# Products of 64 rows in pairs for QKV, output projection and the first FFN layer

## The chip, the core and the metric

The kernel runs on one core of a Trainium2 chip. The metric is the device time of one execution in microseconds. In the runs before the change the median was 483.98 us (two runs, 482.85 and 485.1).

A core has these engines: TensorE (PE in the profile; its weight loads are listed apart, as PEld), VectorE (DVE), ScalarE (ACT), GpSimd (POOL) and SyncE (SP), which here issues nearly all DMAs. TensorE multiplies a stationary operand, which a weight load puts into its array, with a moving operand that streams through, and adds the products up in banks of PSUM. The rows of the array are the contraction: 128 of them, which can be used as one group, as two of 64, or as four of 32.

## What is computed

One transformer layer over 2048 tokens of width 576, all tensors in bf16:

- x is normalised over its width (no gain, no offset) and multiplied with wq, wk, wv (576x576 each). There are 32 heads of 18.
- The tokens form four segments of 512. Inside a segment attention is causal: `softmax(q k^T * 18^-0.5 + mask) v`. In addition each segment reads a memory M, z that is built from all segments before it, with `phi(t) = t+1 if t>0 else exp(t)`: `a_mem = phi(q) M / (phi(q) z + 1e-6)`. Output of a head: `g * a_mem + (1-g) * a_dot`, with `g = sigmoid(beta)`.
- `h = x + o @ wo`.
- `out = h + gelu(layernorm(h) @ w1 + b1) @ w2 + b2`, with w1 576x4608 and w2 4608x576.

576 is four and a half times 128.

## The kernel before

**Tiles and streams.** Tokens are cut into 8 chunks of 256 (`NCH`, `Q`), each of two tiles of 128. Python generators describe the work of each stage; each yields what it has to wait for (`need`, L336) and then queues operations with `op` (L112):

- `stream_P(tl)` (L347, one for each of the two tiles): load x, layernorm (L303), transpose the normalised tile into `xT` (by TensorE for the first two chunks, by DMA afterwards), QKV in four blocks of 432 columns (L372 to L392), then the transposes of q and k.
- `stream_M` (L434): the memory of a chunk.
- `stream_A` (L565): attention in 80 visits. In a visit `scores` (L481) makes 16 products in groups of 32 rows into the four PSUM banks `st4`, ScalarE takes one exponential over all four banks into a buffer `pt` (L495), GpSimd masks (L499), and `weighted` (L510) multiplies with the values into the bank `ox` (L518). The value products of a visit are queued behind the scores of the next one.
- `stream_B(tl)` (L610): transpose the attention output `o_nat`, output projection in two blocks of 288 columns, add x, layernorm, transpose into `xn2T`.
- `stream_F1` (L690): the first FFN layer. For each pair of 128 hidden units one bank takes two blocks of 256 tokens (five products each), then DVE copies the bank to `hT` (L733). ScalarE's gelu follows over many units at once (L741).
- `stream_F2` (L748): the second FFN layer, 36 products of 288 columns into one bank (L767).

**A contraction over 576.** `mm5` makes it in five products, the last one with 65 live rows:

```
for k in range(4):
    nc.tensor.matmul(out=out_ap, lhsT=lhsT_of(slice(0, P), k), rhs=rhs_of(slice(0, P), k), start=(k == 0), stop=False)
nc.tensor.matmul(out=out_ap, lhsT=lhsT_of(slice(0, KTAIL), 4), rhs=rhs_of(slice(0, KTAIL), 4), start=False, stop=True)
```

In the profile the first four are L300 and the last is L301. Row 65 is a row of ones times b1 in the first FFN layer, and zeros elsewhere. QKV, output projection and first FFN layer all go through it.

**Weights.** wq, wk, wv and wo are loaded once (`weights`, L233: one DMA of 512 rows onto 128 partitions and one of 64 rows). w2 stays in SBUF. w1 is loaded anew for each chunk, in 9 groups of 512 columns, into two buffers (five for the first chunk): `load_w1` (L675) issues three DMAs per group, 512 KB, 64 KB and the 1 KB row of b1, when the group two before it has been used.

**Banks.** PSUM has eight banks here: four in `st4` for the scores, `ox`, and three that P, B, M, F1 and F2 share through `Slots` (L154). `ox` joins these three before and after the attention.

**What sets the order.** A planner in the kernel (L64 to L152, L776 to L819) plays the whole program through at build time, with a duration for each operation, a rate for DMA, and a due time from the table `SLACK` (L69). DVE, ACT, POOL and SP take the operation that is ready and due first. TensorE takes the first stream that is ready, in the order `stream_B`, `stream_A`, `stream_P`, `stream_M`, then F1 and F2, whichever is behind (L794 and L795); when the FFN lags, it comes first. What results is a fixed list of instructions for each engine, each queue in order; on the chip nothing is reordered. While F1 hasn't begun and TensorE has nothing to do, the planner puts in filler products (L805).

## Time and profile before

| what | value |
|---|---|
| median of the runs | 483.98 us (482.85 to 485.1) |
| profiled execution, first to last instruction (span) | 481.9 us, 2.1 us less than the median; what lies around the span is not in the profile |
| TensorE busy | 471.6 us, 98% of the span; mean granted clock 0.996 |
| DVE, ACT, POOL busy | 283.4, 290.0, 206.8 us |
| first FFN layer, QKV, output projection: L300 and L301, products | 308 blocks, 64 blocks, 32 blocks of five |
| score blocks (L489) | 80 of 16 products |
| DMA | 80.97 MB, 67 w1 loads of 512 KB and 5 more into `hT` for the first chunk; 64 transposing DMAs |
| first L300 of the first FFN layer | about 45 us |
| last first-layer product | about 458 us |

The profile is one execution. In the rows for groups a line reads: line of the kernel, engine, operation, output and input by name, shapes, count, then busy time of the group, mean of one, and idle time before them with what ended it. Products overlap in the pipeline, so the mean duration of one is longer than the distance from its start to the next one's. In the timeline each row is a run of equal instructions: start of the first, time to the end of the last, engine, line, shapes, count.

### The profile page before, as it was taken

Reading aid. Unit: us, or ns where it says so; the run is one execution under the profiler, and the core shown is the slowest. Engines: PE = TensorE matmul, PEld = TensorE weight load, DVE = VectorE, ACT = ScalarE, POOL = GpSimd, SP = SyncE. Lnnn points to the kernel's source line nnn. Section 1 sums busy time; section 2 is a strip of 40 time slices with the busy share of each in tenths; the row PEclk is TensorE's granted clock in tenths of the full one; section 3 lists DMA queues with packets and bytes.
Section 4 is the critical chain, followed back from the end, with each engine's and each line's share of the span. In section 5 each row is a group of like instructions: output and inputs, shape, how many; then the busy total and the mean of one; then the engine's idle time right before and its main releaser. Section 6 shows DMA issues by size and latency. Waiting matters only on the chain.

```text
span 481.9 us, 14443 instructions
## 1 busy us (share of the span) xinstructions
PE 471.6 (98%) x6098; PEld 369.1 (77%) x6098; DVE 283.4 (59%) x688; ACT 290.0 (60%) x205; POOL 206.8 (43%) x291
## 2 busy tenths in 40 slices
PE   8999999799999999999999999999999999999997
PEld 5668778467788878676887878768888778888885
DVE  5798776757776647676546654857534643534311
ACT  2678889763786969468237968658546867122210
POOL 6567552666755246776204353677304251100000
PEclk9999999899999999999999999999999999999999
DMA  8993759576894657499854655787854655755411
GB/s 237 291 337 113 172 147 252 112 139 163 164 215 147 167 160 197 107 197 232 191 174 125 168 152 153 160 145 172 221 171 130 149 151 155 194 173 161 135 38 50
DMA packets 117345, 80.97 MB, mean 168 GB/s; under 512 B 56392, under 2 KB 115232, under 8 KB 117280
## 3 DMA queue, kind: packets, MB, share of 16 engines
q1 hardware_dynamic: 117248, 80.04, 65.9%
q8 instruction: 48, 0.79, 0.7%
q14 instruction: 17, 0.14, 0.1%
q0 software_dynamic: 32, 0.01, 0.1%
HBM read 60.10 MB, written 7.08 MB: 139 GB/s over the span
## 4 chain that ended last, share of the span: by engine, by line
PE 88%; DMA 7%; DVE 2%; SPq 1%; ACT 1%; POOL 0%; issue 0%; ACTq 0%; DVEq 0%; POOLq 0%
PE bank L300 36%; PE bank L767 26%; PE bank L301 9%; PE ox L518 6%; PE st L489 5%; DMA xT<-xn 2%; DMA x_p<-in_A_x_dram 2%; PE ox L767 2%; DMA wqkv<-in_A_wv_dram 2%; PE ox L300 1%; DMA w1g<-in_B_b_dram 1%; ACT pt L495 1%; PE bank L447 1%; PE bank L541 1%; PE bank L805 1%; DMA xT<-o_nat 1%
## 5 line engine op out<-in xcount | busy, mean ns | idle before, releaser
L495 ACT ACTIVATE pt<-st 128x2048 bf16<-128x2048 f32 x80 | 150.2, 1878 | 61.9 <-PE st L489 61.6
L767 PE MATMUL bank<-w_sb,hT 128*128 128x288 bf16 x1080 | 155.7, 286 | 0.0
L300 PE MATMUL bank<-xn2T,w1g 128*128 128x256 bf16 (+1 forms) x1040 | 146.3, 269 | 0.0
L733 DVE CAST hT<-bank 128x512 bf16<-128x512 f32 x126 | 86.7, 690 | 86.9 <-PE bank L301 85.8
L767 PEld LDWEIGHTS <-hT 128*128 128x128 bf16 x1152 | 109.6, 98 | 27.9 <-issue 0.8
L499 POOL TENSOR_SCALAR_AFFINE_SELECT pt<-pt 128x512 bf16<-128x512 bf16 x128 | 81.0, 646 | 82.5 <-ACT pt L495 81.9
L300 PEld LDWEIGHTS <-w1g 128*128 128x128 bf16 x1104 | 101.4, 97 | 17.0
L741 ACT ACTIVATE hT<-hT 128x4608 bf16<-128x4608 bf16 (+3 forms) x22 | 65.9, 2996 | 67.1 <-DVE hT L733 67.0
L301 PE MATMUL bank<-xn2T,w1g 65*128 65x256 bf16 (+1 forms) x260 | 70.4, 271 | 0.1
L300 PE MATMUL bank<-wqkv,xT 128*128 128x432 bf16 x252 | 57.2, 349 | 2.6 <-DMA xT<-xn 2.1
L300 PEld LDWEIGHTS <-xT 128*128 128x128 bf16 x384 | 34.8, 98 | 27.1 <-DMA xT<-xn 2.4
L518 PEld LDWEIGHTS <-pt 128*128 128x128 bf16 x1280 | 43.6, 96 | 5.8 <-POOL pt L499 0.2
L518 PE MATMUL ox<-v_aug,pt 128*128 128x19 bf16 x1280 | 45.8, 172 | 0.1
L563 POOL TENSOR_TENSOR o_nat<-t,t 128x288 bf16<-128x288 f32 x24 | 19.6, 815 | 32.4 <-DVE t L562 32.2
L489 PE MATMUL st<-QT,KT 32*128 32x128 bf16 x1280 | 32.2, 217 | 0.7 <-ACT pt L495 0.7
L533 POOL TENSOR_TENSOR pq<-ek,pq 128x512 bf16<-128x512 bf16 x24 | 28.1, 1170 | 10.2 <-DVE ek L531 8.3
L771 DVE TENSOR_TENSOR ot<-bank,hc 128x288 bf16<-128x288 f32 x30 | 13.7, 457 | 30.0 <-PE bank L767 29.2
L489 PEld LDWEIGHTS <-KT 32*128 32x128 bf16 x1280 | 18.6, 92 | 14.7 <-issue 12.9
L301 PEld LDWEIGHTS <-w1g 65*128 65x128 bf16 x276 | 26.9, 97 | 3.5 <-DMA w1g<-in_B_b_dram 0.4
L317 POOL TENSOR_TENSOR rstd_b<-rstd_b,mhalf 128x1 f32<-128x1 f32 x16 | 8.8, 552 | 44.6 <-DVE rstd_b L312 44.6
L383 ACT CAST qk_pad<-bank 128x432 bf16<-128x432 f32 x31 | 15.9, 522 | 16.9 <-PE bank L301 12.6
L637 DVE TENSOR_TENSOR h_t<-bank,x_b 128x288 f32<-128x288 f32 x32 | 14.6, 457 | 13.5 <-PE bank L301 13.1
(99 smaller groups left out, 499.8 us busy)
## 6 DMA issues: line engine op xcount, KB each, us to landing
w1g<-in_B_w_dram SPq DMA_DIRECT2D x67, 512.0 KB
w_sb<-in_B_w_dram SPq DMA_DIRECT2D x6, 864.0 KB
hd<-h_t SPq DMA_DIRECT2D x16, 288.0 KB
hc<-hd SPq DMA_DIRECT2D x32, 144.0 KB
w1g<-in_B_w_dram SPq DMA_DIRECT2D x67, 64.0 KB
x_b<-in_A_x_dram SPq DMA_DIRECT2D x18, 144.0 KB
hT<-in_B_w_dram SPq DMA_DIRECT2D x5, 512.0 KB
out_dram<-ot SPq DMA_DIRECT2D x16, 144.0 KB
```

The lines of the kernel that those rows point to most:

```text
L300: nc.tensor.matmul(out=out_ap, lhsT=lhsT_of(slice(0, P), k), rhs=rhs_of(slice(0, P), k), start=(k == 0), stop=False)
L301: nc.tensor.matmul(out=out_ap, lhsT=lhsT_of(slice(0, KTAIL), 4), rhs=rhs_of(slice(0, KTAIL), 4), start=False, stop=True)
L383: op("ACT", 0.52, lambda ch=ch, uh=uh, qk=qk: nc.scalar.copy(out=qk[:, 24 * ch:24 * ch + 24, 0:Dh], in_=uh), [b], [(*qkk, ch)])
L489: nc.tensor.matmul(out=st4[:, i, n * P:(n + 1) * P], lhsT=KTs[(c - c % 2 + kt // 2) % 3][rows, g, (kt % 2) * P:(kt % 2 + 1) * P], rhs=QTs[ ...
L495: op("ACT", 1.88, lambda: nc.scalar.activation(out=pt[:], in_=st4[:], func=ACT.Exp, scale=scale), sk, [("pt", slot, n) for n in range(4)], ...
L499: op("POOL", 0.65, lambda n=n: nc.gpsimd.affine_select(out=pt[:, :, n * P:(n + 1) * P], in_=pt[:, :, n * P:(n + 1) * P], pattern=[[0, 4], ...
L518: nc.tensor.matmul(out=oxv[:, 4 * (g % 4) + i, :], lhsT=pts[slot][:, i, n * P:(n + 1) * P], rhs=v_augs[(2 * s0 + kt) % 6][:, 4 * g + i, :] ...
L533: op("POOL", 1.16, lambda: nc.gpsimd.tensor_tensor(out=pq[:], in0=e_g, in1=pq[:], op=ALU.add), ["ek"], ["pq"], slack=SLACK["add"])
L563: op("POOL", 0.8, lambda: nc.gpsimd.tensor_tensor(out=o_dst, in0=t1[:], in1=t2[:], op=ALU.add), ["t1", "t2"], ok, slack=SLACK["sum"])
L733: op("DVE", 0.684, lambda hT=hT, jp=jp, acc=acc: nc.vector.tensor_copy(out=hT[:, 2 * jp:2 * jp + 2, :], in_=acc), [b], [("hT", c % 2, jp)] ...
L741: op("ACT", (f1 - f0) * Q * 0.00083 + 0.18, lambda hT=hT, f0=f0, f1=f1: nc.scalar.activation(out=hT[:, f0:f1, :], in_=hT[:, f0:f1, :], fun ...
L767: nc.tensor.matmul(out=acc, lhsT=hT[:, q, tl * P:(tl + 1) * P], rhs=w2_sb[:, q, hs], start=(q == 0), stop=(q == NF - 1))
```

## The change

- `mm5` goes. Its successor `lanes` makes nine steps of two products, the lower product on partitions 0 to 63, the upper on 64 to 127. Each half has its own result and its own bank: half 0 takes one set of output columns, half 1 another, and both contract over all of 576 in nine pieces of 64 rows. The upper half takes the pieces in another order of storage (`xs`).
- For this, xT and xn2T hold each 64-row piece of the transposed activations on both halves (9 slots of 128 columns where there were 5). The tile to be transposed gets its first 64 columns once more behind its last (`layernorm` writes twice, POOL copies for `o_nat`), and each DMA transpose becomes two, of 5 and of 4 blocks (`spread_t`); where TensorE transposes, ACT copies the even slots and DVE twice the odd ones (`spread`).
- QKV becomes three pairs of 288 columns (q on half 0 and k on half 1, twice, and v in two halves), the output projection one pair, the first FFN layer a pair for each 256 of 512 hidden columns. The biases b1 are no row of the product any more; the eviction adds them (`tensor_tensor` in place of `tensor_copy`).
- w1 is loaded by two DMAs of 288 KB, each onto 64 partitions, with rows of 512 bytes where they had 1024. The other weights are laid out in the same way.
- The four score banks may be taken by the other streams. A visit of attention begins when all four are free.
- The planner knows a tiling for each operation (32, 64 or 128) and adds 0.095 us where it changes; its choice for TensorE is by tiling (below). Nearly all of `SLACK` has new values.
- `pt` has two buffers for three, xn2T three for four. The load of x and the layernorm of the next chunk are queued when the current tile has been transposed. The gates of beta are computed earlier.

Second FFN layer, scores, value products, gelu and memory stay.

The core of the diff:

```diff
+    def lanes(outs, weight, moving):
+        for k in range(KB):
+            for h in range(2):
+                xs = k if h == 0 else (k - 1) % KB
+                nc.tensor.matmul(out=outs[h], lhsT=weight(half(h), k, xs), rhs=moving(half(h), k, xs), start=(k == 0), stop=(k == KB - 1))
...
+        def apply():
+            for to, n in ((0, D), (D, HB)):
+                nc.vector.tensor_scalar(out=dst[:, to:to + n], in0=src[:, 0:n], scalar1=mv[:, 0:1], scalar2=rstd[:],
+                                        op0=ALU.subtract, op1=ALU.mult)
...
+    def spread(bank, b, dst, key):
+        pt = bf16v(bank[:])[:, 0:KT * P].rearrange("p (k q) -> p k q", q=P)
+        op("ACT", 0.69, lambda: nc.scalar.copy(out=dst[:, 0:KB:2, :], in_=pt), [b], [key])
+        for h in range(2):
+            op("DVE", 0.4, lambda h=h: nc.vector.tensor_copy(out=dst[half(h), 1:KB:2, :], in_=pt[half(1 - h), h:h + 4, :]), [b], [(*key, h)])
+
+    def spread_t(dst, src, rd, wr, slack):
+        for o in range(2):
+            n = KT - o
+            dma_t(n, dst[:, o:KB:2, :], src[:, o * HB:o * HB + n * P], rd, wr[o:o + 1] if o == 0 else wr[1:], slack)
...
+            for pr in range(3):
+                wk = ["wq", "wk"] if pr < 2 else ["wv0", "wv1"]
+                xk3 = [kx, (*kx, 0), (*kx, 1)]
+                yield need(None, bank_slots, xk3 + wk, mode=64, n=2)
+                bs = [bank_slots.take() for _ in range(2)]
+                accs = [banks[b][:, 0:NH] for b in bs]
+                op("PE", KB * mm(NH), lambda pr=pr, accs=accs, xTt=xTt: lanes(
+                    accs, lambda r, k, xs: xTt[r, xs, :], lambda r, k, xs: wqkv[r, k, pr * NH:(pr + 1) * NH]), xk3 + wk, bs, mode=64)
...
+        def again():
+            if gh == 0:
+                o_t = o_nats[c % 2][:, qt, :]
+                op("POOL", 0.2, lambda: nc.gpsimd.tensor_copy(out=o_t[:, D:XW], in_=o_t[:, 0:HB]), ok, [("oe", c % 2, qt)], slack=slack if c < 2 else SLACK["sum"])
...
-        dma(512, lambda: nc.sync.dma_start(out=wt[:, 0:4, :], in_=B_w1[0:512, fcols].rearrange("(k p) f -> p k f", p=P)), (), [k], SLACK["w1"])
-        dma(64, lambda: nc.sync.dma_start(out=wt[0:64, 4, :], in_=B_w1[512:576, fcols]), (), [k + ("t",)], SLACK["w1"])
-        dma(1, lambda: nc.sync.dma_start(out=wt[64:KTAIL, 4, :], in_=b1_row[:, fcols]), (), [k + ("b",)], SLACK["w1"])
+        for h in range(2):
+            f0 = n % NG * 512 + h * Q
+            dma(288, lambda h=h, f0=f0: nc.sync.dma_start(out=wt[half(h), :, :], in_=B_w1[:, f0:f0 + Q].rearrange("(k r) f -> r k f", r=HB)),
+                (), [(*k, h)], SLACK["w1"])
...
+                for a in range(2):
+                    if a:
+                        yield need(mode=64)
+                    op("PE", KB * mm(Q), lambda accs=accs, a=a, wt=wt, c=c: lanes(
+                        [acc[:, a, :] for acc in accs], lambda r, k, xs: wt[r, k, a * P:(a + 1) * P],
+                        lambda r, k, xs: xn2T[c % NX][r, :, xs, :]), xks[0] + xks[1] + wk, bs, mode=64)
+                for h in range(2):
+                    f = 4 * fg + 2 * h
+                    op("DVE", 0.69, lambda hT=hT, f=f, acc=accs[h]: nc.vector.tensor_tensor(
+                        out=hT[:, f:f + 2, :], in0=acc, in1=bias(f, Q), op=ALU.add),
+                       [bs[h], "b1T"], [("hT", c % 2, f // 2)], slack=SLACK["evict"])
+                    bank_slots.give(bs[h])
...
+        if free_at["PE"] <= now:
+            best = {}
+            for g in [*first, *ffn]:
+                if g in waits and waits[g].idle and waits[g].mode not in best and waits[g]() <= now:
+                    if g is ffn[1] and work["F1"] > 0 and g is F1 and 64 in best:
+                        continue
+                    best[waits[g].mode] = g
+            if lead and 32 in best and len(best) > 1:
+                del best[32]
+            if best:
+                inside = now - entered
+                if tiling == 64:
+                    order = (64, 32, 128) if inside < SLACK["in64"] else (32, 64, 128)
+                elif tiling == 128:
+                    order = (32, 128, 64) if inside < SLACK["in128"] else (32, 64, 128)
+                else:
+                    order = (64, 128) if came == 128 else (128, 64)
```

In the new table `in64` is -53, so from the 64-row tiling scores are taken as soon as they are ready, and `in128` is 2.5 us.

## The prediction

> **What bounds the kernel now.** I read the page's busy shares first, then the chain that ended last, then the busy times by stage, and last the order of TensorE's instructions in a few microseconds. From the page:
>
> ```profile
> PE 471.6 (98%) x6098; PEld 369.1 (77%) x6098; DVE 283.4 (59%) x688; ACT 290.0 (60%) x205; POOL 206.8 (43%) x291
> ...
> PE 88%; DMA 7%; DVE 2%; SPq 1%; ACT 1%; POOL 0%; issue 0%; ACTq 0%; DVEq 0%; POOLq 0%
> ...
> L300 PE MATMUL bank<-xn2T,w1g 128*128 128x256 bf16 (+1 forms) x1040 | 146.3, 269 | 0.0
> ```
>
> TensorE is busy 98% of the span and holds 88% of the chain; no other engine passes 60%. Busy time alone could hide waits, so the stages come next (columns: length, then busy time of PE, PEld, DVE, ACT, POOL, clock, DMA share):
>
> ```profile
> 24.00:100.00 76.00, 72.17 (x1199) 55.01 (x1198) 57.92 (x142) 60.86 (x48) 42.52 (x60) 0.98 0.71 184
> 100.00:200.00 100.00, 100.00 (x1405) 78.20 (x1403) 67.40 (x170) 70.04 (x51) 58.24 (x81) 1.00 0.71 170
> 200.00:300.00 100.00, 99.92 (x1292) 77.73 (x1281) 57.84 (x142) 63.57 (x43) 43.23 (x56) 1.00 0.70 168
> 300.00:400.00 100.00, 99.53 (x1326) 78.53 (x1324) 56.96 (x138) 65.94 (x43) 45.85 (x63) 1.00 0.67 161
> ```
>
> From 100 to 400 us TensorE idles 0.55 us. Time taken off its stream there comes off the span, unless something else then comes late. Before about 45 us it is different: the filler products of L805 (70 of them, the last at 42.4 us) show that TensorE waits there for the first attention chunk.
>
> The mean of 269 ns for a product overlaps with its neighbours, so the true price is the distance between starts, from the timeline of PE:
>
> ```profile
> 207.27 0.30 PE L541 MATMUL bank<-MZ_blk,pq 128*128 128x76 bf16 x4
> 207.51 0.40 PE L489 MATMUL st<-QT,KT 32*128 32x128 bf16 x16
> 207.84 0.56 PE L518 MATMUL ox<-v_aug,pt 128*128 128x19 bf16 x16
> 208.26 0.89 PE L300 MATMUL bank<-wqkv,xT 128*128 128x432 bf16 x4
> 208.99 0.35 PE L301 MATMUL bank<-wqkv,xT 65*128 65x432 bf16 x1
> 209.17 0.60 PE L300 MATMUL bank<-xn2T,w1g 128*128 128x256 bf16 x4
> 209.61 0.27 PE L301 MATMUL bank<-xn2T,w1g 65*128 65x256 bf16 x1
> 209.72 0.60 PE L300 MATMUL bank<-xn2T,w1g 128*128 128x256 bf16 x4
> ```
>
> From 209.17 to 209.72 is one FFN block: five products of 256 columns in 0.55 us, the fifth with only 65 live rows but at full price. In the records of single products the steps are 109 ns at 256 columns, 122 at 288, 182 at 432, 55 at 128, and the step after a 65-row product is 4 to 5 ns longer.
>
> The score block (L489) is the only work in row groups. Its sixteen products start in four rounds of four; inside a round the starts lie 4 ns apart, and the last two rounds begin 56 ns after the one before. So four groups run at once, each into its own bank, for what one full product of 128 columns costs (55). It also shows what entering and leaving costs. L541's products stand 34 ns apart, so its four should give way at 207.41, but the scores start at 207.51; and the last score starts at 207.695, needs 56 ns, and L518 follows at 207.84. That is 96 ns in and 91 out (93 to 96 and 91 wherever scores border other work): 80 blocks, 160 switches, 15 us already in the span and counted as busy.
>
> **Part 1, products removed.** A contraction of 576 takes 5 passes now and 9 half passes, two at a time, afterwards (4.5).
> - First FFN layer: 268 blocks of 4x109+113 = 549 ns and 40 blocks of 128 columns of 280 ns, 158.3 us. After: 134 pairs of 9x109 = 981 ns and 20 of 9x55 = 495, 141.4.
> - QKV: 64 blocks of 4x182+187 = 915 ns, 58.6. After: 48 pairs of 9x122 = 1098, 52.7.
> - Output projection: 32 blocks of 4x122+126 = 614, 19.6. After: 16 of 1098, 17.6.
>
> 236.5 becomes 211.7: **24.8 us less**. Four QKV tiles (0.37 us each) and two output projections (0.13) lie in the head, where the chain of the first chunk and not TensorE's load decides: 1.7 us of this is not won, leaving 23.1.
>
> **Part 2, the price of a pair's step.** No 64-row pair runs in the trace. If both halves run like score groups, a step costs a full product plus 1 ns (56 against 55); a second start that isn't hidden costs 4. That is 0 to 7.5 us over 1872 steps. The score row is nearest: +1 ns, **+1.9**. The two-run operand of the first layer (two tiles of 128 columns) I put at nothing within the same bounds.
>
> **Part 3, more switches.** Now every block but the scores has one tiling, and the order between them is free. Afterwards FFN, QKV and output projection stand in the 64-row tiling, second layer and value products in the full one. Each score block must be followed by value products (128) before the next scores, so a stretch between two score blocks that also holds 64-row work has three switches where it had two. The trace has such work in 75 of 79 stretches. The new order in `step` collects one kind of work: after scores it goes to the kind it didn't come from, and it stays in the full tiling for 2.5 us. I take a quarter of the stretches as free of 64-row work, so 60 more there, and 30 more where no scores stand (the tail from 410 to 458 us, now 48 us of first and second layer in turn, and the pauses of 10 to 25 us between score bursts): 90 at 93 ns, **+8.4**. Bounds: 40 more (3.7) if blocks are well collected, 150 (14) if banks and w1's two buffers break them up.
>
> **Part 4, DMA.** The transposes for xT, o and xn2T are each split in two (5 and 4 blocks): 40 more issues of 1.21 us on SP's queue, and about 1.2 us later landing. w1 loses its bias row: 0.38+0.48+0.44 us of issue become two of some 0.48, 24 us less on SP. SP's 250 busy us become about 274, not a bound; but behind each extra transpose wait w1 and x loads. In the chain, xT<-xn holds two pieces (4.2 us at 88 and 5.7 us at 216) and x_p<-x two before them; TensorE stood idle 2.1 us for the first. There 1.2 us more may show twice; against that, the change issues the next chunk's x load and layernorm ahead of the QKV products. I take +0.5 for both together, from -2 (these waits go) to +8 (every landing late at the two places and the tail's loads too).
>
> w1 packets halve to 512 bytes. Median packet times are 18 ns at 256 bytes, 46 at 1024, 51 at 1152, so I estimate 28 at 512: 56 ns for what took 46, 22% more. Now 512 KB move in 1.9 us, and the whole load lands 3.2 us after its issue; then in about 4. In the tail, at today's 4.1 us per group, a buffer is free for two groups less the 2.0 us of its own products, 6.2 us. That covers it; packed closer, at 3 us per group, the 4.0 us left would just do.
>
> A weighed rule: 64 rows written by 64 packets of 1024 bytes (the tail of w1) took 0.25 us at 428.60, 46 ns each, like the full loads' packets. The Trainium skill, SBUF — State Buffer, section "Door 1: The DMA port swizzle", says that 64 rows reach half of the ports and measures 196 GB/s against 328. The trace's small piece doesn't agree (262 GB/s). By the row the sum stands; by the rule it is that of the fourth rival below.
>
> **Part 5, what is hidden.** Evictions with the bias: a PSUM add of 288 columns takes 457 ns (L637), a copy 456, so 690 at 512 as today. Layernorm's second write (32 times 0.15 to 0.3), `spread`'s copies (12 of about 0.4), POOL's 16 copies of about 0.2: beside TensorE, with DVE at 59%. In the head they sit on the chain, about 1 us, against gates moved earlier and two QKV pairs in place of three chunks ahead of the first scores: nothing. Two `pt` buffers suffice: on TensorE's queue the values of visit v-2 stand ahead of the scores of v. Three xn2T buffers too: the transposes of chunk c wait for the first layer of c-3 in place of c-4, and today that is done 49 us before the output projection of c, or more.
>
> **Sum.** -24.8+1.7+1.9+8.4+0.5 = -12.3: a span of 469.6 for 481.9. The runs' median is 483.98, 2.1 above that span; with the same 2.1 around it, **472**.
>
> **Rivals.**
> - *Switches and late landings eat most of it.* 150 switches, pairs at +4 ns, waits +4: -24.8+1.7+7.5+14+4 = +2.4, so 486; at half of the way from the sum above, 479. For: two w1 buffers cap a 64-row stretch at two groups (3.9 us). Against: the score banks add four to the FFN's. 478 to 490, chance 0.24.
> - *More is won.* 40 switches, waits -2, pairs at +0: -24.8+1.7+3.7-2 = -21.4, so 463; 457 to 464. For: the pauses without scores, where 64-row work can be gathered in few stretches. 0.13.
> - *Weight loads don't hide (slower).* In a pair, each half must load 64 rows while it streams. A load with a 19-column product costs 25 ns (L518); one such load open per step is 1872x25 = 47 us: 472+47 = 519. It decides from 12 ns per step (1872x12 = 22 us: the 12 us gain and 2% more). Against: in the scores, loads for a group start 10 ns after that group's product and four fit into a 56 ns round. 0.05. The Trainium skill, TensorE: Matmul & The Clock Gate, "The mechanism" in Part 3, says loads overlap running products only of other row groups; the score records don't agree.
> - *Half loads at half rate.* 576 KB then take about 4.3 us (512 KB now 1.9), 72 x 4.3 = 310 us of the queue beside 180 of others: over 490, some 500. The 46 ns packets speak against it. 0.05. This is where the rule of the Trainium skill's page SBUF — State Buffer would lead.
> - *The pairs don't overlap at all:* 1872 steps twice: over 600. 0.01.
>
> My forecast (464 to 478) keeps 0.52. Two per cent, about what a measurement tells from no change here, is 474.3 to 493.7. Faster: 0.13 and 0.40 of the forecast's 0.52, 0.53; slower 0.09 (unhidden loads 0.05, 0.03 of the half loads, the last 0.01); within, the other 0.38. Range 460 to 488: it leaves out some 0.07 below and 0.12 above.
>
> **What would show it.** The first layer's steps at 109 to 110 ns with two products each; the scores' neighbours still at 93 ns per switch; 220 to 310 switches in all; TensorE without gaps from 100 us on; the fillers ending near 42 us. Wrong if a pair's step is 115 ns or more, if w1 or xT appear among PE's waits with more than 5 us, or if switches pass 310.

## The result and the profile after

The changed kernel takes **555.68 us** (median of two executions, 555.14 to 556.22) against 483.98: 1.148 times the time before, with an interval of 1.143 to 1.153. The forecast was 472, the range 460 to 488. Span: 553.4 us against 481.9.

The page of the changed kernel: TensorE's row and the row of the clock, the row of the DMA engines in tenths, the hardware DMA queue (packets, MB, share of 16 engines' time), and the shares of the chain that ended last.

```profile
PE 490.8 (89%) x8049; PEld 378.8 (68%) x8049; DVE 290.5 (53%) x745; ACT 292.0 (53%) x225; POOL 207.7 (38%) x300
...
PEclk8999998799999899989999999999989799989999
DMA  8993989988499984986998986998875867997631
...
q1 hardware_dynamic: 181504, 85.22, 83.9%
...
PE 61%; DMA 13%; DVE 10%; ACT 5%; issue 4%; SPq 4%; POOL 2%; DVEq 0%; ACTq 0%; POOLq 0%
```

Before, TensorE was busy 98% of the span and held 88% of the chain. Now it is busy 89% and holds 61%; the shares of transfers (13%), VectorE (10%) and ScalarE (5%) have grown from 7, 2 and 1%, so TensorE waits. The queue's row says where to look first. Before, it read `q1 hardware_dynamic: 117248, 80.04, 65.9%`: the same data but for 6%, in 1.55 times as many packets, which keep the sixteen engines busy for 464 us (83.9% of 553.4) in place of 318. The row of tenths has slice after slice at 8 and 9.

The three stretches in which TensorE had 0.55 us without work before (length; busy time of PE, PEld, DVE, ACT, POOL; granted clock; DMA share; GB/s):

```profile
100.00:200.00 100.00, 84.40 (x1282) 63.87 (x1283) 55.45 (x135) 51.09 (x41) 37.27 (x50) 0.95 0.90 154
200.00:300.00 100.00, 88.98 (x1540) 70.06 (x1537) 59.07 (x159) 56.30 (x46) 50.01 (x71) 0.98 0.91 153
300.00:400.00 100.00, 92.71 (x1527) 71.50 (x1524) 49.75 (x119) 63.51 (x44) 39.21 (x55) 1.00 0.86 171
```

TensorE is idle 34 us of these 300. The DMA share was 0.71, 0.70 and 0.67 and is near 0.9, while the rate was 170, 168 and 161 GB/s and is 154, 153 and 171: the engines are busier and move about as much. What TensorE waited for (us in total, times, longest), by the page's view of waits:

```profile
PE bank L339 <- DMA w1g<-in_B_w_dram: 13.1, 12, 2.4
PE bank L339 <- DMA xT<-o_nat: 4.6, 4, 3.1
PE st L339 <- DMA xT<-o_nat: 3.6, 1, 3.6
PE bank L368 <- DVE xn L360: 3.5, 1, 3.5
PE st L339 <- DVE qk_pad L443: 3.2, 2, 2.6
PE bank L339 <- issue: 2.9, 2, 2.2
PE st L339 <- ACT qk_pad L441: 2.6, 4, 1.1
PE st L339 <- DMA w1g<-in_B_w_dram: 2.5, 4, 1.0
PE st L339 <- DVE hT L802: 2.2, 3, 0.8
```

L339 is the pair. All rows of this view together are 24.5 us for transfers, 20.5 for VectorE, 6.6 for ScalarE, 1.2 for GpSimd and 5.0 for "issue" (no cause that the profile shows); before they were 4.5, 1.5 and 0.7, and none for the last two. So there are two families: transfers that land late, and work of VectorE and ScalarE that isn't done in time, much of it the emptying of banks.

And the pairs themselves, in order of time:

```profile
303.78 0.40 PE L539 MATMUL st<-QT,KT 32*128 32x128 bf16 x16
304.11 2.14 PE L339 MATMUL bank<-xn2T,w1g 64*128 64x256 bf16 x36
306.18 0.56 PE L568 MATMUL ox<-v_aug,pt 128*128 128x19 bf16 x16
```

Thirty-six products of 256 columns, 18 steps of two, from 304.11 to the switch before 306.18: 109 ns a step. Over all steps inside pairs the median distance is 109 ns at 256 columns and 122 at 288, what one full product costs. The pairs do what they were made for.

**The account.** To see where 71 us went I price the distances between starts on TensorE, as the prediction did: a step by the distances measured there (55, 109, 122 and 182 ns at 128, 256, 288 and 432 columns, that is 0.417 ns a column plus 2.4 ns; 25 ns for the products of 19 columns), a switch 94 ns; a longer distance is a wait, and one about twice its price, inside a run of equal products, is the halved clock. In us:

| | products and fillers | switches | waits | halved clock, missing records | rest | first to last start |
|---|---|---|---|---|---|---|
| before | 445.9 | 160: 15.0 | 9.3 | 2.2 | 4.7 | 477.1 |
| after | 431.4 | 286: 26.9 | 73.9 | 12.9 | 3.5 | 548.5 |
| difference | -14.5 | +11.9 | **+64.6** | **+10.7** | -1.2 | +71.4 |

The halved clock goes with the waits. In the records of the clock the kernel before has one stretch at 0.5 before its end (3.4 us), the changed kernel eight, of 3.4 or 6.8 us. Each of the eight begins during a wait of TensorE or within 2 us of its end; these waits are 0.6 to 3.6 us long. Not every long wait has one: behind 3.1 us that end at 172.4 there is none for 12 us. One of the eight, in the tail:

```profile
487.94 3.44 PE L339 MATMUL bank<-xn2T,w1g 64*128 64x256 bf16 x35 [2.40 <-DMA w1g<-in_B_w_dram]
```

After 2.40 us without work this row (35 products) takes 3.44 us, where the 36 products at 304.11 took 2.14. This late load cost its wait and some 1.3 us more behind it.

### The profile page after: what moved, and what is told of

It is laid out like the page before. It is cut to its first block, busy times and chain, and to the rows that moved or that the text cites. A ratio compares the mean times of both kernels' runs of the same rounds, so it can differ in the third digit from the quotient of the medians.

```text
span 553.4 us, 18318 instructions
## 1 busy us (share of the span) xinstructions
PE 490.8 (89%) x8049; PEld 378.8 (68%) x8049; DVE 290.5 (53%) x745; ACT 292.0 (53%) x225; POOL 207.7 (38%) x300
## 3 DMA queue, kind: packets, MB, share of 16 engines
q1 hardware_dynamic: 181504, 85.22, 83.9%
## 4 chain that ended last, share of the span: by engine, by line
PE 61%; DMA 13%; DVE 10%; ACT 5%; issue 4%; SPq 4%; POOL 2%; DVEq 0%; ACTq 0%; POOLq 0%
PE bank L339 25%; PE bank L836 17%; DMA w1g<-in_B_w_dram 9%; PE st L339 6%; PE ox L568 4%; PE st L539 3%; ACT pt L545 2%; SPq L150 2%; DMA xT<-o_nat 2%; DVE hT L802 2%; PE ox L836 2%; ACT hT L810 2%; POOL pt L549 1%; PE ox L339 1%; DMA xn2T<-xn 1%
## 5 line engine op out<-in xcount | busy, mean ns | idle before, releaser
L339 PE MATMUL bank<-xn2T,w1g 64*128 64x256 bf16 (+1 forms) x2052 | 142.0, 275 | 15.5 <-DMA w1g<-in_B_w_dram 13.1
L339 PEld LDWEIGHTS <-w1g 64*128 64x128 bf16 x2484 | 120.1, 97 | 48.5 <-DMA w1g<-in_B_w_dram 21.0
L836 PE MATMUL bank<-w_sb,hT 128*128 128x288 bf16 x1044 | 141.8, 286 | 0.7 <-ACT hT L810 0.6
L802 DVE TENSOR_TENSOR hT<-bank,b1T 128x512 bf16<-128x512 f32 x107 | 70.5, 685 | 107.3 <-PE bank L339 98.6
L810 ACT ACTIVATE hT<-hT 128x4096 bf16<-128x4096 bf16 (+4 forms) x26 | 66.6, 2566 | 80.5 <-DVE hT L802 80.3
L339 PEld LDWEIGHTS <-xT 64*128 64x128 bf16 x1152 | 60.2, 97 | 36.6 <-issue 12.8
L339 PE MATMUL bank<-wqkv,xT 64*128 64x288 bf16 x531 | 50.1, 291 | 0.5 <-DMA xT<-xn 0.2
L339 PE MATMUL st<-wqkv,xT 64*128 64x288 bf16 x306 | 31.9, 288 | 8.6 <-DVE qk_pad L443 2.6
L339 PE MATMUL st<-xn2T,w1g 64*128 64x256 bf16 x288 | 25.4, 276 | 5.5 <-DMA w1g<-in_B_w_dram 2.5
L712 POOL TENSOR_TENSOR h_t<-h_t,b_bc 128x576 f32<-128x576 f32 x16 | 20.4, 1276 | 20.5 <-DVE xn L360 19.9
L441 ACT CAST qk_pad<-st 128x288 bf16<-128x288 f32 x19 | 7.2, 402 | 34.4 <-PE st L339 15.6
```

The source lines that it names most:

```text
L339: nc.tensor.matmul(out=outs[h], lhsT=weight(half(h), k, xs), rhs=moving(half(h), k, xs), start=(k == 0), stop=(k == KB - 1))
L712: op("POOL", 1.36, lambda: nc.gpsimd.tensor_tensor(out=h_t[:], in0=h_t[:], in1=b2_bc[:], op=ALU.add), ["b2"], [("h", tl)], slack=SLACK["hb"])
L802: op("DVE", 0.69, lambda hT=hT, f=f, acc=accs[h]: nc.vector.tensor_tensor(out=hT[:, f:f + 2, :], in0=acc, in1=bias(f, Q), op=ALU.add), [bs ...
L810: op("ACT", (f1 - f0) * Q * 0.00083 + 0.18, lambda hT=hT, f0=f0, f1=f1: nc.scalar.activation(out=hT[:, f0:f1, :], in_=hT[:, f0:f1, :], fun ...
L836: nc.tensor.matmul(out=acc, lhsT=hT[:, q, tl * P:(tl + 1) * P], rhs=w2_sb[:, q, hs], start=(q == 0), stop=(q == NF - 1))
```

## The experiments

Most of these kernels keep the changed kernel's written order, instruction by instruction, and change one thing in it; then a difference is that thing's and not another order's. "Waits" and "halved clock" are the columns of the account. The kernel before was run beside each; its single times lie between 483.2 and 487.9, so the ratio is the safer column, and "by ratio" below means a difference of ratios times 484 us. Each experiment ran once. The runs that are not in the table (e2, e3, e6, e9 to e12) stand in the text with their times.

| run | what differs | us | before beside it | ratio | waits | halved clock |
|---|---|---|---|---|---|---|
| (changed kernel) | | 555.68 | 483.98 | 1.148 | 73.9 | 12.9 |
| e1_w1_once | w1 loaded for chunk 0 only | 519.81 | 483.22 | 1.076 | 48.6 | 4.7 |
| e5_w1_rows | w1 on 128 partitions, 1024-byte rows | 535.73 | 486.93 | 1.100 | 60.1 | 9.0 |
| e13_second_once | second transposes once per buffer | 546.07 | 487.85 | 1.119 | 67.9 | 10.0 |
| e14_rows_second_once | the two above together | 522.80 | 487.85 | 1.072 | 50.8 | 5.1 |
| e15_order_again | all work, another order | 544.03 | 487.85 | 1.115 | 58.9 | 11.1 |
| e4_before_split | *before*, w1 split in two ways | 491.54 | 483.22 | 1.017 | 17.0 | 2.3 |
| e8_before_w1_halves | *before*, w1 moved as the change does | 506.20 | 486.93 | 1.040 | 29.8 | 4.2 |

**Is it w1 at all?** Theories: (T1) w1's loads, shorter and on half the partitions, come late; (T2) the second transposes do, 40 more on the same queue; (T3) the order as written is longer. First, w1 is not loaded after chunk 0 (the buffers keep old weights):

```diff
-            dma(288, lambda h=h, f0=f0: nc.sync.dma_start(...), (), [(*k, h)], SLACK["w1"])
+            go = lambda h=h, f0=f0: nc.sync.dma_start(...)
+            dma(288, go if n < NG else lambda: None, (), [(*k, h)], SLACK["w1"])
```

> The changed kernel with the order of every queue kept, but w1 loaded only for the first chunk: the later chunks multiply with whatever the buffers hold (this part of the computation is left out). Theory 1, the half loads of w1 (576 KB in some 3.4 us where the whole took 2.3) fill the transfer queue and hold up all that waits behind them: most of the 70 us goes, below 505 us. Theory 2, the second transposes do it: stays above 535. Theory 3, the written order itself is bad, with banks handed between streams too tightly, whatever the transfers cost: above 535 as well.

519.81 us. Half of the loss (36 us) goes with the reloads, more than T2 or T3 said and less than T1. It doesn't tell bytes from shape, since the kernel before loads the same bytes. But the queue is now busy for 47.6% of the span, less than in the kernel before (65.9%), and VectorE and ScalarE still end 25 us of TensorE's waits: part of the loss is not the transfers' load.

**The second transposes, first run.**

```diff
-        o = op("SP", 1.25, lambda: nc.sync.dma_start_transpose(out=dst, in_=src), rd, wr, slack)
+        o = op("SP", 1.25, lambda: nc.sync.dma_start_transpose(out=dst, in_=src) if blocks != 4 else None, rd, wr, slack)
```

> The changed kernel with the order of every queue kept, but without the second transposes (4 blocks each, 40 of them): the odd slots of xT and xn2T are filled by the first tiles or with zeros and then stay (left out of the computation: the current values of these slots). Theory 2, the transposes: most of the 70 us goes, below 505. Theory 1, w1's halves: 5 to 20 us go, the transposes being some 45 us of transfer time against w1's 77 us more. Theory 3: under 5 us.

551.43 us, only 4 less, the number of theory 3. But this kernel clears the first layer's operand once, 6 us on POOL in the head, and its first scores come at 33.9 us where the changed kernel's come at 24.1. The edit cost 9.8 us in one place and gained in others, so the run does not settle the price; e13 below does.

**The planner told true prices.** The order comes from a planner that takes a w1 half for 0.46 us of issue and 270 GB/s. The trace has 0.60 us and 1.5 to 2 us for 288 KB.

```diff
-        return transfer(op("SP", 0.46, issue, rd, wr, slack), kb, 1.66, rd, wr)
+        return transfer(op("SP", 0.70 if kb == 288 else 0.55, issue, rd, wr, slack), kb * (1.64 if kb == 288 else 1.0), 1.66, rd, wr)
...
-        return transfer(o, blocks * 32, 1.4, rd, wr)
+        return transfer(o, blocks * 50, 1.4, rd, wr)
```

> The changed kernel, but its planner is told what the transfers cost in the profile: 0.70 us for the issue of a w1 half and 1.75 us for its transfer, 0.92 us for a transpose of five blocks, 0.55 for other issues. The table of due times stays. Theory 3 in the form that the order is bad because it was written with too fast transfers: a clear gain, 515 to 540 us. Theory 1, the transfers themselves are too many for any order: 540 to 560.

562.13 us with 303 switches: above both ranges. The due times in `SLACK` belong to the old prices; with new prices alone the planner's own reckoning is 534. The prices have to change together with the due times (e15).

**What does the shape cost by itself?** In the kernel before, the 512 KB of a w1 load were split, by partitions in even groups and by columns in odd ones:

```diff
+                if n % 2 == 0:
+                    nc.sync.dma_start(out=wt[64 * h:64 * h + 64, 0:4, :], in_=src[64 * h:64 * h + 64, :, :])
+                else:
+                    nc.sync.dma_start(out=wt[:, 0:4, 256 * h:256 * h + 256], in_=src[:, :, 256 * h:256 * h + 256])
```

> The kernel before, with the 512 KB load of each w1 group cut in two transfers: for even groups by partitions (0 to 63 and 64 to 127, rows of 1024 bytes), for odd groups by columns (128 partitions, rows of 512 bytes). It shows which of the two makes the change's half loads slow. If it is the 64 partitions, even groups need 3 us or more for the 512 KB against 1.9, and odd ones some 2.1. If it is the short rows, the other way round. The time should stay within 2% of 484 us, since the loads of this kernel have several us to spare.

From the DMA records, first packet to last, medians: unsplit 1.93 us; by partitions, 1024-byte rows, 2.45 (1.36 and 1.21 for the two); by columns, 512-byte rows on all partitions, 2.88 (1.41 and 1.44). The time of the kernel stayed inside the expected 2%, and neither guess about the load came out as it was put: both shapes cost, the short rows more than the half of the partitions. The cut in two is in both figures, and no run cuts the load and keeps rows and partitions. The packets of 512 bytes took 27 ns in the median, close to the 28 that the prediction estimated; and yet the transfer took 49% longer, not 22.

Then both at once, as the change moves it (values land in other places of the buffer):

```diff
+            for h in range(2):
+                f0 = fg * 512 + h * Q
+                nc.sync.dma_start(out=wt[64 * h:64 * h + 64, 0:4, :].rearrange("r k (s f) -> r k s f", f=Q),
+                                  in_=B_w1[0:512, f0:f0 + Q].rearrange("(k s r) f -> r k s f", r=64, s=2))
```

> The kernel before, its order and products kept; only the 512 KB of each w1 load are moved as the change moves them: two transfers of 64 partitions with rows of 512 bytes (values land in other places). Halving by partitions alone made 2.45 us of 1.9, halving the rows alone 2.88. T1, short rows and half the partitions add up: 3.2 to 3.6 us for both, and the time rises by 2 to 5% (493 to 508), less than the change lost, since this order has the loads further ahead of their products. T2, the two do not add (as in the changed kernel's undisturbed loads, 1.50 us for a half): 2.9 to 3.1 us, 488 to 496. T4, w1's shape alone explains the changed kernel's loss: over 530.

512 KB took 2.99 us (T2's range: the two do not add), and the kernel **506.20** (T1's range): 4% for the shape of one load, in an order in which nothing else had changed. Its waits (us, times, longest):

```profile
PE bank L300 <- DMA xT<-o_nat: 7.9, 7, 2.9
PE bank L300 <- DMA w1g<-in_B_w_dram: 5.9, 10, 1.2
PE ox L300 <- DMA wqkv<-in_A_wk_dram: 2.1, 1, 2.1
PE bank L301 <- DMA w1g<-in_B_w_dram: 1.7, 3, 0.8
```

The largest row is not w1 but a transpose (`xT<-o_nat`), which goes through the same queue and was not touched. In the kernel before it read:

```profile
PE bank L300 <- DMA xT<-o_nat: 1.3, 2, 0.9
```

A slower transfer is paid by others in its queue too.

**The reverse, in the changed kernel:** w1 in one transfer of 128 partitions and 1024-byte rows, and two of 32 KB for the last 64 rows.

```diff
+                if h == 0:
+                    nc.sync.dma_start(out=flat[:, 0:2048]..., in_=B_w1[0:512, fg:fg + 512].rearrange("(k p) f -> p k f", p=P))
+                else:
+                    nc.sync.dma_start(out=flat[0:64, 2048:2304], in_=B_w1[512:576, fg:fg + Q])
+                    nc.sync.dma_start(out=flat[64:128, 2048:2304], in_=B_w1[512:576, fg + Q:fg + 512])
```

> The changed kernel with its written order kept; only the shape of the w1 loads differs: a group's 576 KB come as one transfer to all 128 partitions with rows of 1024 bytes (512 KB) and two of 32 KB for the last 64 rows, in place of two of 64 partitions with rows of 512 bytes. The bytes land in other places of the buffer, so the products take wrong numbers; their count, size and order are the same. T1, the shape of the loads makes them late: near the run with w1 loaded once (519.81), 515 to 530, and TensorE's waits (74 us in the changed kernel) fall by 25 to 40. T2, the reloads cost by their bytes and their place in the order, not their shape: over 540. T3, the waits that are left when w1 is out of the way lie in the written order itself (its own reckoning has 30 us of idle TensorE, against 7 for the kernel before): waits stay above 30 in any case.

535.73 us, 20 less (23 by ratio); the queue's busy share falls from 83.9% to 71.6%, with the same bytes. T3 holds, waits are still 60. T1 was some 6 us too hopeful in the time, and waits fell by 14 where it said 25 to 40. What the shape gives here is about what it cost in the kernel before (19 us).

> As the run with w1 in rows of 1024 bytes, and the second transpose of each pair left out too (the odd pieces of the transposed operands are not written; the buffers of the first layer's operand are zeroed once). T1, transfers are all that holds the order back: 495 to 510, near the 492 that the order reckons for itself, with waits of 30 to 40. T2, transfers by shape matter little: over 530. The order's own idle time (T3) would show as a floor: not under 490.

This is e5 without the second transposes, made as in their first run: 529.85, far above T1 and at the edge of T2. Its head has the same delay as that run (first scores at 33.2), so it tells nothing beyond e14 (below).

**The head.** The first scores start at 24.13 us, before at 16.75; TensorE's fillers end at 59.8 us, before at 42.4. VectorE waited for the gate's beta ahead of the first layernorm, so I issued the gate later:

```diff
-        for o in sorted(ops, key=lambda o: (o.start, o.made)):
+        for o in sorted(ops, key=lambda o: (o.start + 9 * (o in late), o.made)):
```

> The changed kernel, its order and work kept, except that the gate's instructions (one on ScalarE, seven on VectorE) are issued 9 us later in the order. In the changed kernel VectorE waits 2.8 us for the gate's beta before it starts the first layernorm (6.85 us, against 3.50 in the kernel before); TensorE then idles 3.5 us and its next products run at half clock; the first scores come at 24.1 us against 16.75. T1, the gate ahead of the layernorm is the cause: statistics near 3.5 us, first scores near 20, the time 3 to 5 us less (551 to 553). T2, the weights or the two pairs are what comes late in the head: first scores stay past 23, time within 1 us of 555.7.

558.33 us, and T1 falls. The statistics did start at 3.41 us, but the first scores at 25.0, as T2 said (the time is 2.6 us from 555.7, where T2 had 1). The timeline of TensorE in this run and, after it, in the kernel before:

```profile
9.63 0.28 PE L343 MATMUL bank<-wqkv,xT 64*128 64x288 bf16 x1
12.34 0.28 PE L343 MATMUL ox<-wqkv,xT 64*128 64x288 bf16 x1 [2.43 <-DMA wqkv<-in_A_wk_dram]
```

```profile
9.81 0.89 PE L300 MATMUL ox<-wqkv,xT 128*128 128x432 bf16 x4 [0.72 <-DMA wqkv<-in_A_wk_dram]
```

A pair is Q on one half and K on the other, so the first one needs both weights, and wk, on 64 partitions, lands at 12.3 us; before it landed at 9.8, and Q's product had run at 8.0. wv is there for the products at 15.5 (before 12.1). So the start of the head is bound by weights that land later, which the gate's delay had covered. That is 4.3 of the 8.3 us by which the first scores are late here. The other 4 lie between the first products and the scores: six pairs (both tiles' QKV, 108 products), transposes and fillers stand there in the changed order, where the kernel before had six blocks of five.

The head also shows what 64 partitions cost without a cut and without short rows. By the DMA records, first packet to last, wq's 576 rows of 1152 bytes took 2.62 us in the kernel before (512 rows onto 128 partitions, then 64) and 3.97 in the changed kernel (one transfer onto 64 partitions).

**Transposes, again.** This kernel was to leave out the second transposes after each buffer's first use. It leaves out more than its expectation says, the first ones too: 18 of 80 halves are still issued.

> The changed kernel with its order kept, but the second (four-block) transposes are issued only for the first use of each buffer and then left out, so the odd pieces of xT and xn2T stay old (the result is not the reference's). This repeats the earlier run without second transposes (551.43), in which POOL cleared 7 KB per partition in the head for it and the first scores came 9.8 us later than in the changed kernel. T1, the second transposes cost what that run hid: 555.7 - 4 - 9.8 = 541.6, so 538 to 545. T2, the delay in the head was absorbed later and the transposes cost next to nothing: 549 to 553.

534.99, below both ranges. It is the price of 62 transposes (21 us), of which the kernel before has half as well, so neither theory is tested. The next two runs leave out the same.

> The gate later, no second transposes after each buffer's first use, and w1 in rows of 1024 bytes on 128 partitions, all three with the changed kernel's order and products (not the reference's result, as in the runs that have these parts). T1, the costs add: 555.7 less 20 for the rows (measured), 14 for the transposes (T1 of the run before this) and 4 for the gate (T1 of the first): 514 to 521. T2, they overlap, each taking a wait that another leaves in place: 525 to 535. T3, the order itself, which reckons 492 with 30 us of idle TensorE, is the floor: not under 497, and the waits that are left are over 30 us and are evictions (VectorE, ScalarE), not transfers.

520.75: T1's range, but not by T1's sum, since 62 transposes are missing and the late gate had gained nothing. Taken as what it is, it shows a floor: the queue is busy 59.3%, less than before the change, and 49.8 us of waits stay. 15.9 us of them in the page's view are VectorE's, 7.8 ScalarE's, 11.5 transfers'.

**Evictions.** On top of that run the evictions of QKV and of the first layer were cut short (shown for the first layer):

```diff
-                        out=hT[:, f:f + 2, :], in0=acc, in1=bias(f, Q), op=ALU.add),
+                        out=hT[:, f:f + 2, 0:wd], in0=acc[:, :, 0:wd], in1=bias(f, wd), op=ALU.add),
```

> The kernel of the run with all three (520.75), its order kept, and the evictions of the QKV and first-layer banks cut short: from the seventh tile on, 2 of 18 columns per head; from chunk 2 on, 32 of 256 columns per block (the rest of qk_pad, v_aug and hT stays old, so the result is not the reference's). The products are untouched. In that run TensorE waited 15.9 us for VectorE and 7.8 for ScalarE, against 1.5 and 0.7 in the kernel before, and 11.5 for transfers. T1, pairs that need two free banks wait for evictions (L441, L443 and L802 of the changed kernel), and that is what is left of the loss: VectorE's and ScalarE's waits fall under 10 together, and the time to 500 to 510. T2, the eviction is only the last to come, and a transfer or the order's next item is right behind: over 516, with the waits moved to transfers.

513.47 us: between both expectations. 7 us (9 by ratio) belong to the length of evictions; VectorE's and ScalarE's waits fell only from 23.7 to 18.5. In the rows that are left the exponential (`st <- ACT pt`, 3.5 us) is the largest of these two engines, and the others are many and small; what stands ahead of them in their queues was not followed up.

**Transposes, as meant:** the first of each pair always, the second only for a buffer's first use.

```diff
+            seen.setdefault(wr[0][:3], []).append(o)
+            dma_t(n if o == 0 or len(seen[wr[0][:3]]) <= 2 else -n, dst[:, o:KB:2, :], ...)
```

> The changed kernel with its order kept; of each pair of transposes the first is always issued, the second only for the first use of each buffer (the odd pieces stay old after that, so the result is not the reference's). The earlier run meant for this (534.99) left out both after the first use: 18 of 80 pair halves were still issued, so its 21 us are the price of 62 transposes, of which the kernel before has 31 too. T1, the second transposes cost about half of that or more: 541 to 548. T2, they cost next to nothing beside the first ones: over 551.

546.07 us: T1. Leaving out 31 of the 40 second transposes, 128 KB each, saves 10 us (14 by ratio).

> The run before this with w1 in rows of 1024 bytes on 128 partitions as well: its transfers are then those of the kernel before but for one or two small ones per w1 group. T1, what is left over the kernel before (484) is products (-14), switches (+12) and the waits of the order: if the two prices add, 555.7 - 20 - 11 = 524, so 519 to 529. T2, they overlap: 530 to 536.

522.80 us: T1. 20 and 10 add up to what both give together (33). **These are the transfers' part, as far as shape and number go.** This run moves nearly what the kernel before moves (81.2 MB for 80.0) and is still 7% slower. Its transfers are not quite those of before: wq, wk, wv and wo keep their new layout, from 60 to 100 us the DMA share is 1.00, and the same 512 KB load takes 2.55 us in the median where it took 1.93. Its stretches and its waits:

```profile
100.00:200.00 100.00, 91.05 (x1520) 71.06 (x1520) 60.05 (x146) 56.99 (x46) 41.78 (x56) 1.00 0.73 160
200.00:300.00 100.00, 92.08 (x1632) 73.26 (x1626) 63.13 (x168) 63.03 (x50) 51.19 (x72) 1.00 0.73 161
```

```profile
PE bank L340 <- DMA w1g<-in_B_w_dram: 4.4, 4, 2.0
PE st L340 <- DMA xT<-o_nat: 2.9, 1, 2.9
PE st L340 <- ACT qk_pad L445: 2.6, 4, 1.1
PE st L543 <- ACT pt L549: 2.4, 6, 0.9
PE st L340 <- DVE hT L814: 2.2, 3, 0.8
```

In these two stretches the DMA share is 0.73, close to before (0.71, 0.70), the clock is full, and TensorE is still idle 8 or 9 us of each hundred. Over the whole run VectorE (16.1 us) and ScalarE (7.6) end most of the waits, mostly under 1 us each, and transfers 11.1; before, VectorE and ScalarE had 2.2 together.

**The order.** All the work and all the transfers of the changed kernel, but another order: the planner with the prices of the trace, and the table of due times searched anew with them (most entries of `SLACK` changed).

> All the work, transfers and products of the changed kernel (this one computes the reference); only the order is another. The planner is told what the trace shows of transfers (a half of w1 0.70 us to issue and 1.75 us to move, a block of a transpose 0.19 us) and its table of due times was searched anew with these prices; by its own reckoning the order takes 505 us with 324 switches, where the old table with the same prices took 534 and ran in 562. T1, much of the loss is an order written for transfers that do not exist: 525 to 542. T2, the transfers are the bound whatever the order: 550 or more. T3, the new order gains as much as it reckons and no more stays: 505 to 515.

544.03 us, 12 less (16 by ratio) with 38 switches more: 2 us above T1's range, inside it by ratio, and clear of T2 and T3. It takes 39 us more than its reckoning of 505; the old table with the same prices took 28 more than its own (534, e3). An order written for these prices wins back about a sixth of the loss. The DMA share from 100 to 400 us stays near 0.9 (0.95, 0.85, 0.93), but what ends the waits has changed. The two largest rows:

```profile
PE st L340 <- ACT qk_pad L442: 5.9, 10, 1.0
PE bank L340 <- DMA w1g<-in_B_w_dram: 5.3, 6, 1.6
```

All together, transfers end 8.6 us here (24.5 in the changed kernel), VectorE 23.8 and ScalarE 11.7. With as much to transfer as in the changed kernel, most of the waits are now evictions and other work of these two engines. Whether late transfers hold these engines up in turn was not traced.

## Why the prediction failed, step by step

- **Part 1, products (-24.8).** Right. The steps are 109 and 122 ns (56 for the 180 of 128 columns), so 1962 steps (the prediction's sums have as many; its "1872" is a slip) take 212.0 us where the old blocks took 236.5. The account shows only 14.5 because 116 fillers run in place of 70 (+5.1), because some pairs stand as two steps in the records (+3.6), and because the old blocks' 4 to 5 ns after a 65-row product are in its rest.
- **Part 2, the pair's step (+1 ns).** Right within a nanosecond; the rivals of loads that don't hide and of pairs that don't overlap are out.
- **Part 3, switches (90 more, 8.4 us).** 126 more, 11.9 us: 3.5 us too low, inside its bounds (40 to 150); a switch still costs 93 to 96 ns.
- **Part 4, transfers and waits (+0.5, from -2 to +8).** This is the step that failed. It had the longer landings covered by the buffers' window. The runs show that w1's shape costs 20 us (e5; 19 the other way round, e8) and the second transposes 10 (e13), together 33 with their part of the halved clock (e14). Three readings went wrong in it.
  - First, "22% more" came from the time of single packets, 56 ns for what took 46. The packet estimate was right in the kernel before's order (27 ns in e4 and e8; 40 in the changed kernel) and useless: 512 KB went from 1.93 us to 2.99, 55%. 1024 packets of 512 bytes took 2.88 us on 128 partitions and 2.99 on 64, in two transfers each; why so long for packets of 27 ns stays open.
  - Second, the small piece from which I took that half the partitions cost nothing had 64 packets. Its 0.25 us leave out the last packet's own time (0.29 to its end, 223 GB/s), and it was among the fastest: the 72 such pieces took 0.48 us in the median. 256 KB on 64 partitions took 1.21 to 1.36 us, 193 to 217 GB/s, against 272 for the full load, and wq on 64 partitions took 3.97 us where it had taken 2.62. The Trainium skill, SBUF — State Buffer, section "Door 1: The DMA port swizzle", gives 196 GB/s for 64 rows and 328 for 128, at 1 MiB. The medians for 64 rows agree with the first figure; the full load here reached 272 and not the second. I had preferred the row with the least weight. The rival built on that rule (half rate, 500 us) was the nearest to what happened, with too small a chance and price; but 512 KB took 2.99 us and not twice 1.93, and short rows alone made 2.88.
  - Third, the buffer's window (6.2 us for a landing in 4) was reckoned for a queue with nothing else in it. The landing took 4.9 in the median, and the queue is shared: e8's largest wait is a transpose that had not changed.
- **Part 5, what is hidden (0).** Also wrong. In the head the first scores come 7.4 us later. The gates that were moved earlier kept VectorE waiting for beta, weights on 64 partitions and a first pair that needs two of them cost about as much (e9), and six pairs stand ahead of the first scores, not the two that the prediction counted. Elsewhere work of VectorE and ScalarE that lay beside TensorE does so no longer: the waits for them are 27 us against 2, and 24 of them stay with nearly the transfers of before (e14). "DVE at 59%" is a share and says nothing of when. A likely reason, of which only the length of evictions was tested (7 us, e12): a pair needs two free banks at once, both are full at the same moment, so their evictions (0.69 us each for the first layer) follow one another; and 64-row work is collected, so they come in bursts.
- **What the order has in it.** The planner's reckoning of its own order has 30 us of idle TensorE, against 7 for the kernel before, and takes 492 us (e6): 20 above the forecast, even with prices for transfers that were too low. Forecasting from the old trace, I kept the old order's cover ("TensorE without gaps from 100 us on") for an order that I hadn't. Of e14's 39 us over the kernel before, waits are +41.5, the halved clock +2.9, switches +11.9, products -15.8 and the rest -1.4.
- **Halved clock (+10.7).** No step had it. The trace of before shows it once, at 93 us, after the longest wait there (2.1 us).

The signs that the prediction named came out as follows: steps of 109 ns, switches at 93 ns and 286 of them (220 to 310) right; no gaps from 100 us on and fillers near 42 us wrong; w1 and xT among the waits with more than 5 us, named as what would prove it wrong, are there: 15.6 and 8.2.

Open: how the order's 40 us split between the three tilings that must be collected, the two banks a pair takes at once and the score banks lent to pairs (which the scores then wait for). Short evictions took 7 of them. A kernel that doesn't lend the banks was not run, nor one that keeps three `pt` and four xn2T buffers. Nor was the "issue" idle time (5.0 us in three stretches, none before) traced to a cause.

## What to carry to other kernels

A layout that suits TensorE is paid for at the queue: before splitting an operand by partitions, measure its transfer whole, first packet to last, and count everything that stands behind it in that queue. A gain on an engine that is busy 98% is worth its full size only as long as nothing else is late; here the products' steps won 25 us, and waits and the halved clock that goes with them cost 75 more than before. And an order planned with prices is only as good as the prices: after a change of layout, they have to be measured again before the order is planned.

## What the runs showed of the hardware

- 512 KB into SBUF, first packet to last: 1.93 us (128 partitions, rows of 1024 bytes), 2.45 (two of 64 partitions, 1024), 2.88 (128 partitions, 512), 2.99 (two of 64, 512). The disadvantages don't add. All but the first are cut in two transfers.
- 576 rows of 1152 bytes: 2.62 us as 512 rows onto 128 partitions and 64 more, 3.97 in one transfer onto 64 partitions.
- Two 64-row products on the two row halves, each into its own bank, run in the time of one: 109 ns at 256 columns, 122 at 288, weight loads included.
- The changed kernel has eight stretches with a granted clock of 0.5, of 3.4 or 6.8 us. Each begins during a wait of TensorE or within 2 us of its end (waits of 0.6 to 3.6 us); one wait of 3.1 us has none behind it.
